# Agent attention with a gated convolution: one 2560-column DMA transpose for both query units of a pair

## The chip, the cores and the metric

One core of a Trainium2 chip. The metric is the device time of one execution in microseconds; the time shown is the median of three runs.

## The reference

Four batches of 12800 rows with 128 channels, and 49 agents. Attention runs twice: agents over keys and values give a 49 x 128 matrix per batch, then each query row attends to the 49 agents. The result x goes through a causal convolution of 5 taps (a sum over taps per channel), a sigmoid, a product with `x @ w_val`, and a last projection.

```python
a2k = sm(agents, k);  agent_v = a2k @ v          # sm: scaled scores, softmax over the last axis
q2a = sm(q, agents);  x = q2a @ agent_v
for kk in range(5):
    gate_pre += conv_w[kk] * xp[:, kk:kk + S, :]  # xp: x with 4 zero rows ahead
out = (sigmoid(gate_pre) * (x @ w_val)) @ w_out
```

## The kernel before

`agent_v` is folded with the taps and weights into small stationary matrices (`stat`), so that x itself is never formed. The work on queries goes by units of 1280 rows (40 in all, number g), in five steps:

1. `queries`: score matmuls on TensorE (line 376), a 32x32 block transpose (386) and row maxima (745) on VectorE, subtraction on GpSimd (750), exp on ScalarE (758), sums and normalisation on VectorE (763 to 772). The probabilities of a unit are then written three times in 16 bits into a buffer `pt` of [128, 10, 128]: the high part by ScalarE (779), copies of two thirds of it by GpSimd (784), and the low rest by GpSimd (794).
2. `transposes`: `pt` is turned over, so that the 128 entries of a query row lie along the partitions. The first four units do it on TensorE; units 4 to 39 by a DMA transpose, issued by SyncE (835). Its destination is half of an `x1` buffer. An `x1` buffer holds a segment: two units, 2560 columns, segment s = units 2s and 2s+1. There are four `x1` buffers and four `pt` buffers.
3. `shifts`: two plain DMAs per segment (884, from segment 2 on) copy some rows of `x1` at five column offsets into `x2`. They read both halves of the segment. `halo` (819) copies the last 4 columns of the segment before by GpSimd.
4. `gates` and `values`, by chunks of 512 columns (five to a segment, chunk t belongs to segment t // 5): five matmuls on `x1` (922) and one on `x2` (926) give the gate, two more (949, 953) the value. ScalarE applies tanh (935), VectorE multiplies (962), ScalarE rounds to `hh` (968), GpSimd forms the rest `hl` (973).
5. `project`: three matmuls (992 to 994, the last with `hl`), a scaled copy to `ob` on ScalarE (1006), and an output store per pair of chunks (1021).

Loads of keys, queries and values (369) go through 11 buffers `ld`; a load waits until TensorE has used what lay in its buffer. All loads, stores, shifts and DMA transposes are issued by SyncE, in one queue.

TensorE's order is written out by hand (`order`, line 1088). The order on the other engines and on the DMA queue is set by a planner, `Plan`: each step is added with an engine, a duration, what it reads and writes, and for a DMA the time on the wire (`moved`). `Plan.order` walks through a modelled time and picks the next step of each engine by the longest chain behind it (`tail`). The durations are only used for this order.

Of the kernel before, what the change touches and what calls it, by code (L numbers as in the profile page):

```python
# [10 lines left out]
F16 = mybir.dt.float16  # L11
# [6 lines left out]
P = 128  # L18
# [5 lines left out]
NBLK = 10  # L24
# [5 lines left out]
PAD = 16  # L30
# [10 lines left out]
NPT = 4  # L41
NX = 4
# [25 lines left out]
class Plan:  # L68
# [11 lines left out]
    def add(self, engine, us, fn, reads=(), writes=(), moved=0.0, key=None, urge=0.0):  # L80
        i = len(self.steps)
        need = set()
        for x in reads:
            need |= self.wrote.get(x, set())
        for x in writes:
            need |= self.wrote.get(x, set()) | self.read.get(x, set())
        for x in reads:
            self.read.setdefault(x, set()).add(i)
        for x in writes:
            self.wrote[x], self.read[x] = {i}, set()  # L90
        self.steps.append((engine, us, fn, need, moved, key))
        self.urge.append(urge)
# [84 lines left out]
def tile_agent_attention_gated_conv(  # L177
# [25 lines left out]
    def ring(n, shape, dtype, name, pool=const):  # L203
        return [pool.tile(shape, dtype, name=f"{name}{i}") for i in range(n)]
# [12 lines left out]
    qw = ring(NPT, [P, NBLK, A], F32, "qw")  # L217
    qsm = ring(2, [P, NBLK], F32, "qsm")
    qr = ring(2, [P, NBLK], F32, "qr")
    pts = ring(NPT, [P, NBLK, P], F16, "pt")  # L220
    x1s = ring(NX, [P, PAD + SEG], F16, "x1_")
    x2s = ring(3, [P, SEG], F16, "x2")
    ths = ring(NT_, [P, CH], F32, "th")
# [25 lines left out]
    def bank():  # L249
        turn[0] += 1  # L250
        i = turn[0] % 2
        return sc[i], ("sc", i)
# [13 lines left out]
        out=fold, in0=ident[:, 0:AP_], in1=ident[:, AP_:P], op=ALU.add  # L266
# [246 lines left out]
    def fold_weights(b):  # L513
# [143 lines left out]
        def transposes():  # L657
# [4 lines left out]

        add(
            "pe", 0.6, transposes, [(*w_, n) for n in "derv"] + [(*w_, "g")], [at_w],
            key="m",
        )
# [132 lines left out]
    def on_pe(b, u):  # L799
        g = b * NU + u  # L800
        return g < PE_FIRST or (g < (B - 1) * NU and g % TURN in PE_TURNS)

    def unit_rows(g):
        o = PAD + g % 2 * UNIT
        return x1s[g // 2 % NX][:, o : o + UNIT]
# [21 lines left out]
    def transposes(b, u):  # L827
        g = b * NU + u
        pt = pts[g % NPT]
        p_ = ("pt", g % NPT)  # L830
        if not on_pe(b, u):
            dst = unit_rows(g)
            add(
                "dma", 1.4,
                lambda: nc.sync.dma_start_transpose(
                    out=dst.rearrange("p (n i) -> p n i", i=P),
                    in_=pt.rearrange("p n r -> p (n r)"),
                ),
                [(*p_, n) for n in range(3)], [("x1", g // 2 % NX, g % 2)], 2.4,
            )  # L840
            shifts(b, u)
            return
        ps_, at = bank()
        ps = ps_.rearrange("p a b -> p (a b)").bitcast(F16).rearrange("p (h w) -> p h w", h=2)
        dst = unit_rows(g).rearrange("p (h w) -> p h w", h=2)

        def matmuls():
            for n in range(NBLK):
                nc.tensor.transpose(
                    out=ps[:, n // HB, n % HB * P : (n % HB + 1) * P], in_=pt[:, n, :],  # L850
                    identity=ident16,
                )

        add("pe", 0.65, matmuls, [("pt", g % NPT, n) for n in range(3)], [at], key="t")
        add(
            "act", 0.65, lambda: nc.scalar.copy(out=dst[:, 0], in_=ps[:, 0, 0 : HB * P]),
            [at], [("x1", g // 2 % NX, g % 2)],
        )
        add(
            "dve", 0.46,  # L860
            lambda: nc.vector.tensor_copy(out=dst[:, 1], in_=ps[:, 1, 0 : HB * P]),
            [at], [("x1b", g // 2 % NX, g % 2)],
        )
        shifts(b, u)

    def shifts(b, u):

        g = b * NU + u
        if g >= SINGLE and g % 2 == 0:
            return  # L870
        n = 1 if g < SINGLE else 2
        u0 = u + 1 - n
        s = g // 2
        x2, x1 = x2s[s % 3], x1s[s % NX]
        o = (g + 1 - n) % 2 * UNIT
        src = row_keys(s, range(0, g % 2 + 1))
        c = PAD - HALO + o
        for r0, r1, every, us in X2CUTS:
            first = A + (2 if every == 3 else 3 * THREES)
            rows = x1[first : first + 1 + (r1 - r0 - 1) * every : every, c : c + 1]  # L880
            view = [rows.ap[0], (1, TAPS), (1, n * UNIT)]
            add(
                "dma", 0.6,
                lambda r0=r0, r1=r1, rows=rows, view=view: nc.sync.dma_start(
                    out=x2[r0 * TAPS : r1 * TAPS, o : o + n * UNIT],
                    in_=bass.AP(rows.tensor, rows.offset, view),
                ),
                src, [("x2", s % 3, o + i * UNIT, r0) for i in range(n)], us * n,
            )
        if g % 2 and (g + 1) // 2 < B * NU // 2:  # L890
            halo((g + 1) // 2)
# [165 lines left out]
    for b in range(B):  # L1057
        t0 = b * NCH
        for i in range(NU):
            g = b * NU + i + LEAD  # L1060
# [61 lines left out]
    def gate_and_state(t):  # L1122
        state[t] = gates(t)

    run = {
        "k": key_scores, "v": agent_values, "q": queries, "t": transposes,
        "max": lambda b: step(key_max, b), "fold": lambda b: step(fold_weights, b),
        "g": gate_and_state, "a": values, "o": project,
# [58 lines left out]
```

## Time and profile before

| | |
|---|---|
| median of 3 runs | 427.45 us (426.17 to 427.92) |
| span of the profiled execution | 423.6 us |
| its own time | not listed apart from the span; the median lies 3.85 us above the span |
| TensorE busy | 403.9 us (95%) |
| VectorE, ScalarE, GpSimd busy | 293.3, 301.5, 228.2 us |
| bytes moved by DMA | 127.62 MB, mean 301 GB/s |
| DMA transposes (x<-pt) | 36, issued by SyncE |

The span is the time from the first to the last instruction. The page's rows of 40 digits cut it into slices of 10.6 us. In a timeline, the first number is the start and the second the length in us; `SPq` rows are issues on SyncE, and their length is the time of the issue, not of the transfer. In a row of windows, the last three numbers are the granted TensorE clock, the busy share of the DMA engines and GB/s.

### The profile page before, as it was taken

Reading aid. Unit: us, or ns where it says so; the run is one execution under the profiler, and the core shown is the slowest. Engines: PE = TensorE matmul, PEld = TensorE weight load, DVE = VectorE, ACT = ScalarE, POOL = GpSimd, SP = SyncE. Lnnn points to the kernel's source line nnn. Section 1 sums busy time; section 2 is a strip of 40 time slices with the busy share of each in tenths; the row PEclk is TensorE's granted clock in tenths of the full one; section 3 lists DMA queues with packets and bytes.
Section 4 is the critical chain, followed back from the end, with each engine's and each line's share of the span. In section 5 each row is a group of like instructions: output and inputs, shape, how many; then the busy total and the mean of one; then the engine's idle time right before and its main releaser. Section 6 shows DMA issues by size and latency. Waiting matters only on the chain.

```text
span 423.6 us, 10042 instructions
## 1 busy us (share of the span) xinstructions
PE 403.9 (95%) x3907; PEld 197.0 (47%) x3907; DVE 293.3 (69%) x562; ACT 301.5 (71%) x521; POOL 228.2 (54%) x263
## 2 busy tenths in 40 slices
PE   4979999999999999999999899999999989999995
PEld 1358434346555443446555343335555534344443
DVE  3757899867875978667795575767765678676231
ACT  1564568779966777678876486778876567788776
POOL 1002557654657565554566355574366277877553
PEclk9969999999999999999999899999999999999998
DMA  8999999999999999999999999999999977755733
GB/s 320 420 417 411 370 367 353 301 295 310 412 293 283 346 317 362 304 278 356 351 379 324 271 299 370 314 332 302 296 393 322 239 196 161 199 163 176 205 121 124
DMA packets 75129, 127.62 MB, mean 301 GB/s; under 512 B 50466, under 2 KB 50850, under 8 KB 75084
## 3 DMA queue, kind: packets, MB, share of 16 engines
q1 hardware_dynamic: 74940, 126.87, 96.9%
q8 instruction: 30, 0.49, 0.5%
q10 hardware_dynamic: 144, 0.13, 0.2%
q14 instruction: 15, 0.12, 0.1%
HBM read 79.25 MB, written 26.21 MB: 249 GB/s over the span
## 4 chain that ended last, share of the span: by engine, by line
PE 78%; DMA 9%; DVE 8%; ACT 1%; POOL 1%; issue 1%; SPq 0%; POOLq 0%; DVEq 0%; ACTq 0%
PE gate L922 23%; PE sc L376 17%; PE av L480 10%; PE val L949 5%; PE out L992 5%; PE val L953 5%; PE gate L926 5%; PE out L993 4%; DMA ld<-kT 4%; PE out L994 4%; DMA x<-pt 3%; DMA x<-x 2%; DVE h L962 1%; DVE qw L772 1%; DVE qsm L763 1%
## 5 line engine op out<-in xcount | busy, mean ns | idle before, releaser
L973 POOL TENSOR_TENSOR hl<-h,hh 128x512 f16<-128x512 f32 (+1 forms) x101 | 116.9, 1158 | 96.1 <-ACT hh L968 96.0
L922 PE MATMUL gate<-x,stat 128*128 128x512 f16 (+1 forms) x500 | 125.2, 380 | 0.2 <-ACT th L935 0.2
L962 DVE SCALAR_TENSOR_TENSOR h<-th,val 128x512 f32<-128x512 f32 x100 | 67.8, 678 | 66.8 <-PE out L993 26.2
L376 PE MATMUL sc<-ld,ag_sb 128*32 128x320 f32 x1280 | 101.5, 447 | 7.6 <-DMA ld<-kT 7.0
L935 ACT ACTIVATE th<-gate,unscale 128x512 f32<-128x512 f32 x100 | 68.3, 683 | 33.3 <-PE gate L926 31.7
L1006 ACT ACTIVATE ob<-out,oscale 128x512 f32<-128x512 f32 x98 | 67.3, 687 | 21.3 <-PE out L994 20.1
L922 PEld LDWEIGHTS <-stat 128*128 128x128 f16 x505 | 46.3, 97 | 63.7 <-issue 14.8
L968 ACT CAST hh<-h 128x512 f16<-128x512 f32 (+1 forms) x101 | 61.5, 609 | 17.2 <-DVE h L962 16.4
L750 POOL TENSOR_TENSOR qw<-sT,qmx 128x490 f32<-128x490 f32 x40 | 41.4, 1035 | 47.6 <-DVE qmx L745 47.5
L376 PEld LDWEIGHTS sc<-ld,ag_sb 128*32 128x32 f32 x1280 | 36.7, 111 | 59.4 <-issue 25.7
L480 PE MATMUL av<-ld,eT 128*32 128x129 f32 (+1 forms) x1400 | 50.7, 279 | 1.0 <-DVE eT L386 1.0
L480 PEld LDWEIGHTS av<-ld,eT 128*32 128x32 f32 (+1 forms) x1400 | 47.1, 117 | 7.5 <-issue 2.5
L794 POOL TENSOR_TENSOR pt<-qw,pt 128x490 f16<-128x490 f32 x40 | 44.8, 1120 | 3.1 <-ACT pt L779 2.9
L471 ACT ACTIVATE e<-ks,kbias 128x320 f32<-128x320 f32 x80 | 39.3, 554 | 5.4 <-DVE eT L386 3.3
L386 DVE STREAM_TRANSPOSE sT<-sc 128x640 f32<-128x640 f32 x40 | 33.6, 839 | 13.4 <-PE sc L376 12.7
L402 ACT COPY ks<-sc 128x640 f32<-128x640 f32 x40 | 27.7, 691 | 21.2 <-PE sc L376 19.1
L386 DVE STREAM_TRANSPOSE eT<-e 128x640 f32<-128x640 f32 x40 | 33.5, 842 | 9.8 <-ACT e L471 5.2
L926 PE MATMUL gate<-x,stat 95*128 95x512 f16 x100 | 38.3, 383 | 1.5 <-DMA x<-x 1.5
L949 PE MATMUL val<-x,stat 128*128 128x512 f16 x100 | 38.2, 382 | 0.8 <-DVE h L962 0.6
L953 PE MATMUL val<-x,stat 95*128 95x512 f16 x100 | 38.1, 381 | 0.0
L994 PE MATMUL out<-hl,wo 128*128 128x512 f16 x98 | 37.0, 378 | 1.1 <-POOL hl L973 1.1
L992 PE MATMUL out<-hh,wo 128*128 128x512 f16 x98 | 37.3, 381 | 0.1
(130 smaller groups left out, 389.4 us busy)
## 6 DMA issues: line engine op xcount, KB each, us to landing
ld<-kT SPq DMA_DIRECT2D x40, 640.0 KB
ld<-qT SPq DMA_DIRECT2D x40, 640.0 KB
ld<-vP SPq DMA_DIRECT2D x39, 645.0 KB
outT<-ob SPq DMA_DIRECT2D x48, 512.0 KB
x<-x SPq DMA_DIRECT2D x18, 375.0 KB
x<-x SPq DMA_DIRECT2D x18, 100.0 KB
outT<-ob SPq DMA_DIRECT2D x3, 256.0 KB
x<-x SPq DMA_DIRECT2D x4, 187.5 KB
```

The source lines that it names most:

```text
L376: nc.tensor.matmul(out=out[g * BLK : (g + 1) * BLK, j, 0:GT], lhsT=ag_sb[:, b, j * BLK : (j + 1) * BLK], rhs=src[:, g * GT : (g + 1) * GT] ...
L386: nc.vector.transpose(out=out.rearrange("p n (j i) -> p j n i", j=2), in_=in_.rearrange("p j (n i) -> p j n i", i=BLK),)
L480: nc.tensor.matmul(out=av[o + j : o + j + cols, 0 : C + 1], lhsT=et[:, n, j : j + cols], rhs=vt[:, n, :], start=(u == 0 and n < 2), stop=( ...
L922: nc.tensor.matmul(out=pg, lhsT=stat[:, k, :], rhs=x1[:, c : c + w], start=(k == 0), stop=False,)
L926: nc.tensor.matmul(out=pg, lhsT=stat[0 : TAPS * X2R, TAPS + 1, :], rhs=x2[0 : TAPS * X2R, o2 : o2 + w], start=False, stop=True,)
L935: lambda: nc.scalar.activation(out=th, in_=pg, func=AF.Tanh, scale=unscale[:, 0:1]),
L949: nc.tensor.matmul(out=pv, lhsT=stat[:, TAPS, :], rhs=x1s[(b * NCH + n0 // CH) // 5 % NX][:, PAD + o2 : PAD + o2 + w], start=True, stop=False,
L953: nc.tensor.matmul(out=pv, lhsT=stat[0 : TAPS * X2R, TAPS + 2, :], rhs=x2[0 : TAPS * X2R, o2 : o2 + w], start=False, stop=True,)
L962: lambda: nc.vector.scalar_tensor_tensor(out=h, in0=th, scalar=1.0, in1=pv, op0=ALU.add, op1=ALU.mult),
L968: "act", 0.16 + 0.42 * scale, lambda: nc.scalar.copy(out=hh, in_=h),
L973: lambda: nc.gpsimd.tensor_tensor(out=hl, in0=h, in1=hh, op=ALU.subtract),
L1006: lambda: nc.scalar.activation(out=ob[:, o : o + w], in_=po, func=AF.Copy, scale=oscale),
```

## The change

The two `pt` buffers of a pair become two halves of one buffer `ptp` of [128, 2, 10, 128]. The even unit issues no transpose; the odd one issues a single DMA transpose of all 2560 columns into the whole `x1` buffer. It reads all three parts of both units and writes both halves. In the planner it has 2.6 us of issue (1.4 before, for each of two) and 3.6 us on the wire (2.4 before, for each of two). Shifts, gates and `halo` are as before.

```diff
-    pts = ring(NPT, [P, NBLK, P], F16, "pt")
+    ptp = ring(NPT // 2, [P, 2, NBLK, P], F16, "pt")
+    pts = [t[:, h] for t in ptp for h in range(2)]
...
         if not on_pe(b, u):
-            dst = unit_rows(g)
+            if g % 2 == 0:
+                return
+            s = g // 2 % NX
+            pair = ptp[g // 2 % (NPT // 2)]
             add(
-                "dma", 1.4,
+                "dma", 2.6,
                 lambda: nc.sync.dma_start_transpose(
-                    out=dst.rearrange("p (n i) -> p n i", i=P),
-                    in_=pt.rearrange("p n r -> p (n r)"),
+                    out=x1s[s][:, PAD:].rearrange("p (n i) -> p n i", i=P),
+                    in_=pair.rearrange("p h n r -> p (h n r)"),
                 ),
-                [(*p_, n) for n in range(3)], [("x1", g // 2 % NX, g % 2)], 2.4,
+                [("pt", i % NPT, n) for i in (g - 1, g) for n in range(3)],
+                [("x1", s, 0), ("x1", s, 1)], 3.6,
             )
             shifts(b, u)
             return
```

Five lines come into the file, so line 835 becomes 839, 884 becomes 889, 1021 becomes 1026, and 369 becomes 370. TensorE's order is the same row for row. On the other engines the planner, fed with the new step, sets a new order in parts. Names below: `ld` are load buffers, `x_0` to `x_3` the `x1` buffers, other `x` the `x2` buffers; in the new kernel a `pt` is the buffer of a pair.

SyncE's queue at segment 2 (units 4 and 5), the first with DMA transposes, before:

```order
L369 DMA ld_70<-qT 128x1280
L835 DMA_TRANSPOSE x_2_103<-pt_97 128x10x128
L369 DMA ld_71<-vP 128x1290
L835 DMA_TRANSPOSE x_2_103<-pt_98 128x10x128
L369 DMA ld_61<-vP 128x1290
L1021 DMA outT<-ob_121 128x1024
L369 DMA ld_62<-vP 128x1290
L884 DMA x_107<-x_2_103 75x1x2560
```

and now:

```order
L370 DMA ld_70<-qT 128x1280
L370 DMA ld_71<-vP 128x1290
L370 DMA ld_61<-vP 128x1290
L839 DMA_TRANSPOSE x_2_101<-pt_97 128x20x128
L1026 DMA outT<-ob_119 128x1024
L370 DMA ld_62<-vP 128x1290
L370 DMA ld_63<-qT 128x1280
L889 DMA x_105<-x_2_101 75x1x2560
```

The transpose moved behind two value loads, and one more load (`ld_63`) stands between it and the shifts.

The same queue at segment 9 (units 18 and 19), before:

```order
L835 DMA_TRANSPOSE x_1_102<-pt_99 128x10x128
L369 DMA ld_71<-kT 128x1280
L835 DMA_TRANSPOSE x_1_102<-pt_100 128x10x128
L1021 DMA outT<-ob_123 128x1024
L369 DMA ld_61<-kT 128x1280
L369 DMA ld_62<-qT 128x1280
L884 DMA x_105<-x_1_102 75x1x2560
L884 DMA x_105<-x_1_102 20x1x2560
L835 DMA_TRANSPOSE x_2_103<-pt_97 128x10x128
```

and now:

```order
L370 DMA ld_71<-kT 128x1280
L370 DMA ld_61<-kT 128x1280
L839 DMA_TRANSPOSE x_1_100<-pt_98 128x20x128
L1026 DMA outT<-ob_121 128x1024
L370 DMA ld_62<-qT 128x1280
L370 DMA ld_63<-kT 128x1280
L889 DMA x_103<-x_1_100 75x1x2560
L889 DMA x_103<-x_1_100 20x1x2560
L370 DMA ld_64<-qT 128x1280
```

Two key loads stand ahead of the transpose, a key load more ahead of the shifts (`ld_63`), and no transpose directly behind them. At segment 4 two loads more stand ahead of the shifts.

GpSimd's queue at unit 32, near 330 to 341 us of the profile, before:

```order
L784 TENSOR_SCALAR pt_97<-qw_89 128x10x30
L794 TENSOR_TENSOR pt_97<-qw_89,pt_97 128x10x49
L819 COPY x_0_101<-x_3_104 128x4
L973 TENSOR_TENSOR hl_117<-h_111,hh_114 128x512
L973 TENSOR_TENSOR hl_118<-h_112,hh_115 128x512
L541 TENSOR_TENSOR gw<-avT,moe_sb 128x245
```

and now:

```order
L785 TENSOR_SCALAR pt_97<-qw_89 128x10x30
L795 TENSOR_TENSOR pt_97<-qw_89,pt_97 128x10x49
L978 TENSOR_TENSOR hl_115<-h_109,hh_112 128x512
L820 COPY x_0_99<-x_3_102 128x4
L978 TENSOR_TENSOR hl_116<-h_110,hh_113 128x512
L542 TENSOR_TENSOR gw<-avT,moe_sb 128x245
```

The halo copy, which reads the end of the segment before, moved behind the first of the two `hl`.

## The prediction

> **What bounds the kernel now.** I read the head of the page first, then the waits of the matmul engine, then the chain of waits around the one long wait, then the sync engine's timeline.
>
> ```profile
> span 423.6 us, 10042 instructions
> PE 403.9 (95%) x3907; PEld 197.0 (47%) x3907; DVE 293.3 (69%) x562; ACT 301.5 (71%) x521; POOL 228.2 (54%) x263
> PEclk9969999999999999999999899999999999999998
> DMA  8999999999999999999999999999999977755733
> PE sc L376 <- DMA ld<-kT: 7.0, 4, 6.1
> PE gate L926 <- DMA x<-x: 1.5, 1, 1.5
> PE out L994 <- POOL hl L973: 1.1, 1, 1.1
> ```
>
> TensorE is busy for 95% of the span, so it is the bound. The 7.0 us on key loads are the start, which the change leaves alone; TensorE waits for no load after it. Behind it there are two waits of over 1 us: 1.5 us on a shift copy and 1.1 us on GpSimd's `hl`. The DMA row says something else that matters here: for 32 of 40 slices the wire is full as well. It seldom stops TensorE, since loads run far ahead; it reaches TensorE only where a transfer is wanted soon after it is issued. That is the path of this change: transposes, then shifts, then the gate matmul L926. The 1.5 us lie there, in segment 9 (units 18 and 19):
>
> ```profile
> 220.73 7.50 DMA x<-pt
> 228.28 7.34 DMA x<-x
> 235.67 0.39 PE gate L926
> 236.89 2.24 PE gate L922 x5
> ...
> 243.56 1.19 PE gate L922 x5
> ```
>
> The second transpose is issued at 220.73, has landed 7.50 us later, the shifts go out at 228.28, and land 7.34 us after that. The five gate matmuls behind the wait take 2.24 us, those at 243.56 take 1.19. The granted clock says why:
>
> ```profile
> 237.00:240.40 3.40, 3.40 (x9) 1.17 (x8) 1.99 (x7) 1.30 (x2) 1.84 (x3) 0.50 1.05 335
> ```
>
> The eighth column is the clock: 0.50 for 3.4 us after the 1.5 us wait, so half of 3.4, 1.7 us, is lost beside it. The 1.1 us wait of L994 was followed by no such spell (in the page's clock row the only 8 behind the start and ahead of the end is slice 23, 233 to 243.6 us; 340 lies in a slice with 9). Segment 9 costs 1.5 + 1.7 = 3.2 us today. The sync queue around it:
>
> ```profile
> 212.77 7.23 SPq L835 DMA_TRANSPOSE x<-pt  x1
> 220.10 0.53 SPq L369 DMA_DIRECT2D ld<-kT  x1
> 220.73 2.63 SPq L835 DMA_TRANSPOSE x<-pt  x1
> 223.45 1.47 SPq L1021 DMA_DIRECT2D outT<-ob  x1
> 225.02 0.38 SPq L369 DMA_DIRECT2D ld<-kT  x1
> 225.49 0.73 SPq L369 DMA_DIRECT2D ld<-qT  x1
> 228.28 1.65 SPq L884 DMA_DIRECT2D x<-x  x2
> 213.83 0.45 POOL L784 TENSOR_SCALAR pt<-qw 128x300 f16<-128x300 f32 x1
> ```
>
> The odd unit's buffer is complete at 213.83 + 0.45 = 214.3, yet its transpose is issued at 220.7: the first issue takes 7.23 us, since the queue behind it is full. So what decides the landing is not readiness but the bytes queued ahead, at the wire's rate.
>
> **The change, part by part.** TensorE's order is the same row for row, so its work is unchanged; only its waits can move.
>
> Readiness: the merged transpose of segment 9 can be issued at 214.3 instead of 212.8. The 1.5 us cost nothing, because the wire has 7 us queued at that moment; where that cover is gone they would be paid in full. Issue time: two quiet issues and one wire rate:
>
> ```profile
> 361.24 2.94 SPq L835 DMA_TRANSPOSE x<-pt  x2
> 112.00:120.00 8.00, 8.00 (x84) 3.94 (x83) 5.95 (x10) 6.64 (x13) 6.41 (x7) 1.00 1.02 418
> ```
>
> One merged issue should take about the 2.94 us of two; nothing is won or lost. At 418 GB/s (last column) a load of 128x1280 floats, 0.655 MB, takes 1.6 us. This prices the moves. The order puts one more load ahead of segment 9's shifts (the key load after the query load), so they land 1.6 us later. In segment 2 it is also one load, in segment 4 two. Behind the waiting merged transpose stand an output store and loads; that no load is waited for after the start covers their delay, and without that cover a load late by 1.5 us would be a wait of 1.5 us.
>
> What a transpose costs the wire beyond its bytes is the large term. Stretches from the first to the last transposed packet of a pair, with rows in the order segments 4, 5 (transposes adjacent), 2, 9 (a load between) and 17 (quiet):
>
> ```profile
> 120.90:127.06 6.16, 6.16 (x111) 3.86 (x103) 5.04 (x9) 3.22 (x7) 3.49 (x6) 1.00 1.23 199
> 131.61:137.65 6.04, 6.04 (x113) 4.10 (x102) 4.57 (x13) 2.81 (x6) 4.01 (x4) 1.00 1.23 182
> 77.77:85.69 7.92, 7.92 (x58) 3.06 (x57) 7.08 (x13) 6.55 (x13) 4.72 (x6) 1.00 1.16 289
> 220.04:227.72 7.68, 7.68 (x89) 4.13 (x82) 4.29 (x8) 5.25 (x10) 4.79 (x6) 1.00 1.21 242
> 362.44:365.74 3.30, 3.30 (x21) 1.27 (x23) 1.10 (x2) 2.72 (x6) 3.30 (x4) 1.00 1.12 230
> 120.90:124.50 3.60, 3.60 (x99) 2.70 (x91) 2.86 (x5) 1.64 (x4) 2.73 (x4) 1.00 1.24 223
> ```
>
> Lost time is length x (1 - rate/418): 6.16 x (1 - 199/418) = 3.2 us in segment 4, 3.4 in segment 5, 2.4 in segment 2, 3.2 in segment 9, 1.5 in the quiet one; the mean of the four loaded pairs is 3.1. A merged transpose loses between 1.5 (no partner, no queue) and 3.4 (two in a row under load). The first transpose of segment 4 alone, the last row, loses 3.60 x (1 - 223/418) = 1.7; that is engines coming into step. The second loses as much again, though the engines are in step already; I put that down to the hand-over between two instructions, which the merged one has not. So I take the first one's 1.7 and half the quiet pair's 1.5 for the second half: 2.4 us, 0.7 below the mean, both ends kept. By segment 9 eight pairs have passed: 8 x 0.7 = 5.6 us less on the wire, with ends 8 x 1.6 = 12.8 less and 8 x 0.3 = 2.4 more.
>
> The Trainium skill (DMA: Bandwidth & Descriptors, "Anatomy of one DMA") gives each DMA a fixed 2.0 us, fitted for another issuing path, and its rules for kernel authors say to coalesce. Taken as wire time, that is an estimated 16 us by segment 9; segments 2 and 4 would then not wait, and the sum below would be 1.2 us lower. The row at 112:120, with 418 GB/s through queued DMAs, does not bear it out: beside other transfers a fixed part is hidden.
>
> Now the tight segments, with these rows:
>
> ```profile
> 86.20 1.68 SPq L884 DMA_DIRECT2D x<-x  x2
> 93.97 0.38 PE L926 MATMUL gate<-x,stat 95*128 95x512 f16 x1
> 127.74 1.67 SPq L884 DMA_DIRECT2D x<-x  x2
> 135.69 0.38 PE L926 MATMUL gate<-x,stat 95*128 95x512 f16 x1
> ```
>
> Segment 2: shifts issued at 86.20 land at about 93.5 if they take 9's 7.34 us (an estimate), 0.4 before L926. One load more (+1.6), its own pair losing 2.4 as before (0): they land at 95.1, a new wait of 1.2 us. Ends: 0, if they land faster than 7.34 since no transpose follows them directly any more, and 1.6. Being at the 1.1 us that brought no half-clock spell, I count none; 1.7 if it does.
>
> Segment 4: 127.74 + 7.34 = 135.1, due 135.7. Two loads (+3.2) less what segments 3 and 4 save (2 x 0.7) give 136.9; TensorE, 1.2 late, comes at 136.9. Wait 0, ends 0 and 2.0.
>
> Segment 9: landing at 235.6 + 1.6 - 5.6 = 231.6; TensorE wants it at 235.67 - 1.5 + 1.2 = 235.4. No wait, no spell: -3.2. This holds as long as the eight pairs save over about 1 us together.
>
> The wait of L994 on `hl`:
>
> ```profile
> 338.78 0.19 POOL L819 COPY x<-x 128x4 f16<-128x4 f16 x1 [5.99 <-DMA x<-pt]
> 338.93 2.27 POOL L973 TENSOR_TENSOR hl<-h,hh 128x512 f16<-128x512 f32 x2
> 340.13 0.38 PE L994 MATMUL out<-hl,wo 128*128 128x512 f16 x1 [1.11 <-POOL hl L973]
> ```
>
> GpSimd waits 5.99 us for a transpose before its halo copy, with two `hl` behind it; L994 needs the first. In the new order that `hl` stands ahead of the copy, so the 1.11 us go, unless the second becomes late in turn (the merged transpose lands later). Between 0 and -1.1: I take -0.6.
>
> Other reordering on ScalarE, VectorE and GpSimd keeps each unit's steps within one or two chunks of their places; I cost it at nothing, covered by TensorE's queue of other chunks, and if that cover fails it is a wait like the 1.1 us one. The buffers' second use is tight only at segment 9:
>
> ```profile
> 229.62 0.61 ACT L779 CAST pt<-qw 128x490 f16<-128x490 f32 x1 [0.40 <-DVE qw L772]
> ```
>
> This write into unit 18's old place now needs the whole merged transpose landed; today's second one has by 228.3. One load ahead and 5.6 saved make it 224.3: free.
>
> Sum: +1.2 + 0 - 1.5 - 1.7 - 0.6 = -2.6 us; span 421.0. The shown median, 427.45, lies 3.85 above the profiled span, so 427.45 - 2.6 = 424.9, or -0.6%. What a measurement of this kernel can tell from no change is 0.5%, 2.1 us.
>
> **The rivals.**
>
> Same time: the spell moves instead of going. Segment 2's wait of 1.2 to 1.6 us lies between 1.1 (no spell) and 1.5 (spell). If it draws one, +1.7: 426.6. If besides `hl` stays late, 427.2. For it: the wait sits right at the unknown threshold. Against: its shifts have no transpose behind them any more. 427 as its middle.
>
> Slower: the merged transpose loses more wire time than its two parts. Place: segments 2 to 9, price eight times the difference. Wire and TensorE meet at segment 9: with 3.4 us lost per pair (segment 5's) the shifts land at 235.6 + 1.6 + 2.4 = 239.6, 4.0 later than now, the spell stays, and the buffer's write on ScalarE, due at 229.62, waits for 228.3 + 1.6 + 2.4 = 232.3: 427.45 + 4.0 = 431.4. It decides once a merged one loses 0.1 more than the mean: 1.6 + 8 x 0.1 = 2.4 us. For it: both adjacent pairs above lose the most of all. Against: they are still two instructions.
>
> Faster still: with 1.6 us saved per pair (the quiet end) and shifts landing sooner with no transpose behind them, segment 2 waits 0 and `hl` gives all: -3.2 - 1.1 = -4.3, 423.1. For it: the quiet pair's 1.5 us. Against: the wire is never quiet before slice 33. The Trainium skill's fixed cost (above) points this way.
>
> That nothing changes on the queue is out: the order has 18 transposes of 2560 columns for 36 of 1280.
>
> **How the numbers follow.** Forecast 424.9: 0.34. Faster still, 423.1: 0.09. Same, 427: 0.31. Slower, about 431: 0.26. Faster by over 0.5% is 0.34 + 0.09 = 0.43, within 0.31, slower 0.26. The range goes from 422.0, just below the 423.1 case, to 431.5, the slower case at its priced value; about 2 in 10 lie beyond, mostly above. The likeliest case's own range is 423.5 to 426.
>
> **What would show it.** Right: no wait of L926 on x<-x at chunk 45, no 0.50 clock stretch near 237, a wait near 1 us at chunk 10, shorter stretches of transposed packets (pairs under 5.5 us), no wait of L994 on `hl` near 340. Wrong: the same wait at chunk 45 with later shifts; ScalarE's L779 waiting for x<-pt; new waits of L926 in segments 8 or 14; half-clock stretches at new places.

## The result and the profile after

| | before | after |
|---|---|---|
| median | 426.81 us (425.42 to 427.92, 4 runs) | 438.67 us (438.15 to 439.27, 4 runs) |
| ratio | 1 | 1.0272, 95% interval 1.0229 to 1.0315 |
| span of the profiled execution | 423.6 us | 435.7 us |

The change makes the kernel 2.7% slower, outside the range of the prediction and on the other side of the forecast. Ratios, here and below, leave out single runs that lie over 1.5% above the fastest of their kernel; medians and ranges keep them. The head of the page of the kernel after:

```profile
span 435.7 us, 9982 instructions
PE 404.5 (93%) x3907; PEld 195.3 (45%) x3907; DVE 291.0 (67%) x562; ACT 300.5 (69%) x521; POOL 227.9 (52%) x263
PEclk9989999987999999999999999999999999999999
DMA  8999999999999999999899999999999968555733
```

TensorE is busy for 404.5 us, nearly as before (403.9), so nearly all of the 12.1 us is added waiting. The clock row has a new low place, its 9th and 10th digits, and the start ran faster (8 for 6 in the third digit), which hides the new spell in the busy time. The 8 that stood at the 23rd is gone, since that spell now falls on two slices. The waits of TensorE, in us in total, times and longest:

```profile
PE gate L931 <- DMA x<-x: 10.2, 3, 5.0
PE sc L377 <- DMA ld<-kT: 7.0, 5, 5.9
PE av L433 <- DVE m L426: 2.0, 1, 2.0
PE val L954 <- DVE h L967: 1.4, 1, 1.4
...
PE gate L927 <- ACT th L940: 1.2, 2, 1.1
```

The wait on the shifts has grown from 1.5 us in one piece to 10.2 in three; the wait of L994 (now L999) on `hl` is gone; a wait on the key maximum `m` and one on tanh are new. The third piece, 1.01 us, lies at segment 0 and is not the change's: a second profile of the kernel before has 1.14 us there. The other two, and the waits between them, by TensorE's timeline (start, length, in brackets the wait ahead):

```profile
98.69 0.61 PE L931 MATMUL gate<-x,stat 95*128 95x512 f16 x1 [4.97 <-DMA x<-x]
...
190.78 1.24 PE L927 MATMUL gate<-x,stat 128*128 128x512 f16 x5 [1.05 <-ACT th L940]
...
195.34 0.27 PE L433 MATMUL av<-ident,m 128*2 128x128 f32 x1 [2.01 <-DVE m L426]
...
248.44 0.38 PE L931 MATMUL gate<-x,stat 95*128 95x512 f16 x1 [4.25 <-DMA x<-x]
```

98.69 is chunk 10, the first of segment 2 (93.97 before, 4.7 us earlier); 248.44 is chunk 45, segment 9 (235.67 before, 12.8 earlier). Two windows of the clock, in the columns of the prediction:

```profile
95.64:102.47 6.83, 3.78 (x41) 1.92 (x45) 0.81 (x1) 3.01 (x6) 1.16 (x1) 0.50 1.19 212
249.24:252.65 3.41, 3.41 (x12) 1.50 (x11) 2.07 (x7) 1.07 (x3) 1.54 (x2) 0.50 0.80 160
```

The first is new: 3.78 us of work at half clock, 1.9 lost. The second is the one the kernel before had at 237, moved by 12.2. So 4.7 of the 12.1 us are there at chunk 10, 1.9 follow by its spell, 3.1 come at 190 to 196, and 2.75 (4.25 - 1.5) at chunk 45; the `hl` wait gives 1.1 back, and smaller waits make up the rest (1.4 us on `h` for 0.6 before).

Now the path to chunk 10. SyncE's queue at segment 2, first before, then after:

```profile
73.26 5.94 SPq L835 DMA_TRANSPOSE x<-pt  x1
79.30 0.52 SPq L369 DMA_DIRECT2D ld<-vP  x1
79.94 2.68 SPq L835 DMA_TRANSPOSE x<-pt  x1
82.71 0.53 SPq L369 DMA_DIRECT2D ld<-vP  x1
83.34 0.38 SPq L1021 DMA_DIRECT2D outT<-ob  x1
83.81 0.40 SPq L369 DMA_DIRECT2D ld<-vP  x1
```

```profile
77.06 8.95 SPq L839 DMA_TRANSPOSE x<-pt  x1
86.12 0.51 SPq L1026 DMA_DIRECT2D outT<-ob  x1
86.73 0.38 SPq L370 DMA_DIRECT2D ld<-vP  x1
87.20 0.90 SPq L370 DMA_DIRECT2D ld<-qT  x1
88.19 1.71 SPq L889 DMA_DIRECT2D x<-x  x2
```

Between the last transpose and the shifts stand a store and two loads in both orders; the load more of the new order is the one ahead of the transpose. The shifts are issued at 88.19, 2.0 us later than in this profile of before; the prediction had 1.6 for their delay. This part is not firm: in the nine profiles below whose queue up to there is that of before, the shifts are issued at 86.2 to 88.4. And the merged issue holds SyncE for 8.95 us, and the store and loads behind it are issued at 86.1 to 88.1, right ahead of the shifts; before they went out at 82.7 to 84.2, with 2 to 3.5 us to spare. The stretch from the shifts' issue to their landing, before and after:

```profile
86.20:93.67 7.47, 7.40 (x45) 3.10 (x45) 5.52 (x10) 5.26 (x11) 3.49 (x5) 1.00 1.10 306
```

```profile
88.19:98.64 10.45, 5.45 (x25) 2.09 (x22) 4.84 (x8) 4.96 (x9) 2.71 (x4) 0.86 1.17 263
```

10.45 us instead of 7.47. The wire moved 2.75 MB instead of 2.29, which at 306 GB/s is 1.5 us; the other 1.5 us are the lower rate, 263 GB/s. The length is firm: 10.26 and 10.35 us in two more profiles of this order, 7.15 to 9.15 in the nine with the queue of before. Segment 9, by the chain of waits:

```profile
224.75 13.61 DMA x<-pt
...
238.42 9.97 DMA x<-x
```

The transpose lands at 238.36. TensorE was ready for chunk 45 at 248.44 - 4.25 = 244.19, 5.8 us later; before, the second transpose landed 5.9 us ahead of that point (228.22 and 234.17). So here too the transpose is not late against TensorE; the shifts are, 9.97 us instead of 7.34. This piece is less firm than chunk 10: of three runs below with the same queue at segment 9, two have shifts of 7.5 and 7.6 us there, one of 10.0.

The waits at 190 to 196 begin on GpSimd and pass through ScalarE:

```profile
188.35 0.19 POOL L820 COPY x<-x 128x4 f16<-128x4 f16 x1 [6.87 <-DMA x<-pt]
188.50 1.01 POOL L751 TENSOR_TENSOR qw<-sT,qmx 128x490 f32<-128x490 f32 x1
...
189.54 0.61 ACT L759 ACTIVATE qw<-qw 128x490 f32<-128x490 f32 x1 [4.58 <-POOL qw L751]
```

The halo copy waits 6.87 us for segment 7's transpose, the subtraction of the queries stands behind it, ScalarE's exp waits 4.58 us for that, and tanh and the key copies stand behind the exp.

### The profile page after: what moved, and what is told of

Its sections match the earlier page's. It is cut to its first block, busy times and chain, and to the rows that moved or that the text cites. A ratio compares the mean times of both kernels' runs of the same rounds, so it can differ in the third digit from the quotient of the medians.

```text
span 435.7 us, 9982 instructions
## 1 busy us (share of the span) xinstructions
PE 404.5 (93%) x3907; PEld 195.3 (45%) x3907; DVE 291.0 (67%) x562; ACT 300.5 (69%) x521; POOL 227.9 (52%) x263
## 4 chain that ended last, share of the span: by engine, by line
PE 69%; DMA 22%; DVE 4%; ACT 1%; issue 1%; POOL 1%; SPq 1%; POOLq 0%; DVEq 0%
PE gate L927 20%; PE sc L377 15%; DMA x<-pt 8%; PE av L481 7%; DMA x<-x 6%; DMA ld<-vP 6%; PE val L954 4%; PE gate L931 4%; PE out L997 4%; PE val L958 4%; PE out L998 4%; PE out L999 4%; DMA ld<-kT 2%; DVE h L967 1%; DVE qsm L764 1%
## 5 line engine op out<-in xcount | busy, mean ns | idle before, releaser
L377 PE MATMUL sc<-ld,ag_sb 128*32 128x320 f32 x1280 | 103.0, 451 | 8.0 <-DMA ld<-kT 7.0
L481 PEld LDWEIGHTS av<-ld,eT 128*32 128x32 f32 (+1 forms) x1400 | 45.4, 115 | 9.4 <-issue 3.7
L931 PE MATMUL gate<-x,stat 95*128 95x512 f16 x100 | 38.5, 385 | 10.2 <-DMA x<-x 10.2
L412 DVE TENSOR_REDUCE kmx<-ks 128x2 f32<-128x640 f32 x39 | 31.5, 812 | 8.4 <-ACT ks L403 8.3
```

The source lines that it names most:

```text
L377: nc.tensor.matmul(out=out[g * BLK : (g + 1) * BLK, j, 0:GT], lhsT=ag_sb[:, b, j * BLK : (j + 1) * BLK], rhs=src[:, g * GT : (g + 1) * GT] ...
L481: nc.tensor.matmul(out=av[o + j : o + j + cols, 0 : C + 1], lhsT=et[:, n, j : j + cols], rhs=vt[:, n, :], start=(u == 0 and n < 2), stop=( ...
L931: nc.tensor.matmul(out=pg, lhsT=stat[0 : TAPS * X2R, TAPS + 1, :], rhs=x2[0 : TAPS * X2R, o2 : o2 + w], start=False, stop=True,)
```

## The experiments

Each time is a median, each ratio is against runs of the kernel before on the same chip. "Order" is the order of every engine's instructions.

**Order, instruction and place: three runs.** They tell apart the merged instruction (theory A), the planner's order (B) and the place of the first half (C). The first keeps the order of the kernel after and splits the instruction again:

```diff
-    nc.sync.dma_start_transpose(out=x1s[s][:, PAD:]..., in_=pair...)
+    for h in range(2):
+        nc.sync.dma_start_transpose(out=unit_rows(g - 1 + h)..., in_=pair[:, h]...)
```

> The changed kernel's order on every engine, but at each place of the merged transpose two transposes of 1280 columns back to back, from the two halves of the same buffer. Theory A (the single long instruction delays what is queued behind it): back near the kernel before, 427 to 429 us, with no wait of L926 above 2 us. Theory B (the planner's new order, with a load more between transpose and shifts in segments 2 and 9, is what costs): 437 to 440, the waits at chunks 10 and 45 as in the changed kernel. Theory C (the first half no longer starts before the second unit is ready): 437 to 440 too, since the first half still waits for the second here.

Measured: 438.75 us (434.24 to 442.11), ratio 1.0241 (1.0163 to 1.032). In time the same as merged. The trace is not: TensorE waits 5.26 us at chunk 10, much as merged (4.97), but hardly at chunk 45,

```profile
245.83 0.39 PE L936 MATMUL gate<-x,stat 95*128 95x512 f16 x1 [0.57 <-DMA x<-x]
```

and there are half-clock spells at 195.3 (3.41 us) and 355.7 (6.83 us) and a wait of 2.07 us on tanh instead. The second keeps the order of the kernel before; the planner gets its old two steps, the even one issues nothing:

```diff
     add("dma", 1.4,
-        lambda: nc.sync.dma_start_transpose(out=dst..., in_=pt...),
+        merged,            # the odd unit issues 2560 columns, the even one nothing
         [(*p_, n) for n in range(3)], [("x1", s, g % 2)], 2.4)
```

> The order of the kernel before on every engine, row for row; only the even unit's transpose is gone and the odd unit's place issues the merged one of 2560 columns. Theory A (the instruction): 436 to 440 us. Theory B (the planner's order): 424 to 428. Theory C (the first half starts late): 434 to 440, with the transposes landing later after the odd unit's issue than in the kernel before, where 9's landed 7.5 us after it.

Measured: 431.93 us (431.32 to 435.45), 1.0152 (1.0101 to 1.0204). The third is the second with two transposes at the odd unit's place:

> As the run with the merged transpose in the order of before, but two transposes of 1280 columns back to back at the odd unit's place. Theory A (the instruction): 427 to 429 us, since there is no long instruction. Theory B (the planner's order): 425 to 428. Theory C (the first half starts late): 434 to 440, the same as with the merged one.

Measured: 431.82 us (429.96 to 433.29), 1.0131 (1.0086 to 1.0175). Both times lie between the ranges that I had given to the three theories, above 429 and below 434, so no theory holds alone. The merged instruction is worth nothing that can be seen in either order (438.67 and 438.75; 431.93 and 431.82): A falls. The place of the first half costs 1.3 to 1.5%, some 6 us, and the planner's order another 1.2% by the ratios, some 5 us (6.7 by the medians). Both B and C hold, each for about half. One thing in my expectations was wrong: split, the first half waits only for its own unit, and its place in the queue, not the second unit, makes it late.

The third run shows what the place alone does. SyncE's queue in it at segment 2, and from its chain of waits the shifts:

```profile
75.23 9.63 SPq L841 DMA_TRANSPOSE x<-pt  x2
84.96 0.54 SPq L370 DMA_DIRECT2D ld<-vP  x1
85.59 0.38 SPq L1031 DMA_DIRECT2D outT<-ob  x1
86.06 0.38 SPq L370 DMA_DIRECT2D ld<-vP  x1
86.93 1.69 SPq L894 DMA_DIRECT2D x<-x  x2
```

```profile
86.93 9.31 DMA x<-x
```

Against the kernel before, the first transpose and one value load have changed places, nothing else. The shifts are issued 0.7 us later, and take 9.31 us instead of 7.47; what stands between is issued at 85 to 86.4 instead of 82.7 to 84.2. That fits SyncE's hold as the cause, but it does not show it. The four profiles with a late first half in the order of before have 8.69 to 9.41 us for these shifts, and the nine with the queue of before 7.15 to 9.15: longer on average by 1.2 us, with ranges that overlap. No run takes the hold away by itself. In this trace TensorE waits 2.61 us at chunk 10, with a spell of 6.83 us behind it, and 2.89 us on `hl` at 344.72, with one of 3.41; chunk 45 doesn't wait. So that the first half's place costs some 6 us is shown; by which wait it does so changes from run to run.

**Shifts ahead of what stands between.** The queue of the kernel after, with the store and two loads moved behind the shifts in segments 2 and 9:

> The changed kernel, but in segments 2 and 9 the store and the two loads that stood between transpose and shifts stand behind the shifts. If the shifts are late because of what is queued between (theories A and B, in their part on the queue), they land about 4 us after their issue instead of 10, the waits of L926 at chunks 10 and 45 go, and with them the half-clock spells: 438.7 less 5.0, 4.3 and about 3 of spells is 427 us, with something of it lost again where the wire stands idle. If they are late because the transposes themselves land late (theory C), they still wait at least 2 us each: 434 or more.

Measured: 446.46 us (444.4 to 447.64), 1.0471 (1.0427 to 1.0516): the worst of all. The shifts did land sooner, 6.1 us after their issue in both segments, and the waits at chunks 10 and 45 fell to 0.80 and 0.49 us. But the waits only moved:

```profile
PE gate L935 <- DMA x<-x: 8.3, 4, 5.9
PE out L1001 <- ACT ob L1015: 2.7, 1, 2.7
PE gate L931 <- DMA x<-pt: 2.1, 1, 2.1
```

The longest, 5.9 us, lies at segment 4 now, whose transpose took 14.28 us to land. I read this as a wire that is full anyway, where what is put back comes late for everything behind it; no run isolates that.

**One segment's place.** The order of before, merged in segments 3 to 19 alone, then in segment 2 alone. The first of the two, against the second run above:

```diff
-                if g % 2:
+                if s == 2 and g < 6:    # segment 2: a transpose for each unit, as before
+                    nc.sync.dma_start_transpose(out=unit_rows(g)..., in_=pt...)
+                elif g % 2:
```

> The order of before on every engine, with merged transposes at the odd units' places in segments 3 to 19; segment 2 keeps its two transposes at their old places. If the price of the late first half sits in segment 2 (wait of 2.65 us at chunk 10 and a half-clock spell of 3.4 us that costs 1.7): 431.9 - 4.3 = 427.6 us, and no wait at chunk 10. If it is spread over later segments, the waits at chunk 45 (3.5 us) and on hl (3.9 us) stay and the time is 429 to 432.

Measured: 429.66 us (427.38 to 436.21), 1.0055 (1.0019 to 1.0092).

> The kernel before, order and all, with the merged transpose in segment 2 alone. If the late first half does its harm there (shifts land 2.6 us later, and a half-clock spell behind the wait): 429 to 431 us, with a wait of 2 to 3 us at chunk 10. If not: 426 to 428.

Measured: 428.44 us (426.34 to 430.95), 1.0055 (1.0025 to 1.0086). Segment 2 carries a part: undoing it there gives 2.3 us back by the medians (431.93 to 429.66; 1.0%, some 4 us, by the ratios), doing it there alone costs 2.0 (426.46 beside it), between the two cases expected. My 4.3 is not excluded by the first, but the second is below it, and the wait at chunk 10 didn't go in the first of the two (1.6 us). The rest is elsewhere: that run waits 3.60 us at chunk 45 and 1.27 on `hl`.

**One load in the order.** The kernel after, in segment 2 the last load ahead of the shifts moved behind them:

> The changed kernel with one edit in the queue: in segment 2 the query load that the planner put ahead of the shifts stands behind them. If a load ahead of the shifts costs its wire time there (1.6 us), they land 8.8 us after their issue instead of 10.45, the wait at chunk 10 falls from 5.0 to about 3.3 us, and the time from 438.7 to 436 (437 without, 435 with a shorter half-clock spell). If the shifts are late for what stands directly behind the transpose (the first load took 3.3 us there instead of 1.6), the wait stays above 4.5 us and the time at 438 to 439.

Measured: 435.59 us (434.57 to 438.35), 1.0193 (1.0135 to 1.0252), 3.1 us less. As expected of the load's own wire time:

```profile
97.05 0.39 PE L935 MATMUL gate<-x,stat 95*128 95x512 f16 x1 [3.16 <-DMA x<-x]
```

The wait falls from 4.97 to 3.16 us, and the shifts take 8.75 us. The waits behind it are not those of the kernel after, though: 3.33 us at chunk 20, where there was none, and 0.87 at chunk 45 for 4.25. So the 3.1 us are not the load at chunk 10 alone.

**The planner's two numbers.** The kernel after with two numbers changed:

```diff
-                "dma", 2.6,  ...  3.6,
+                "dma", 9.0,  ...  6.0,
```

> The changed kernel with two other numbers in the planner and nothing else: the merged transpose has 9.0 us of issue and 6.0 us on the wire there, about what the trace of the changed kernel shows under load (2.6 and 3.6 before). If the planner's order is what makes the changed kernel slower than the merged one in the old order, another order moves the time by several us, and with truer numbers down: 428 to 434. If any order with the merged transpose loses the same: 437 to 440.

Measured: 430.31 us (427.56 to 434.03), 1.0061 (1.0022 to 1.01). Two numbers that only set the order are worth 8.4 us. What stood on the shifts is now on loads, which the new order puts later:

```profile
PE gate L931 <- DMA x<-x: 2.5, 2, 1.6
PE av L481 <- DMA ld<-vP: 1.6, 2, 1.4
PE sc L377 <- DMA ld<-qT: 1.4, 1, 1.4
```

**The halo copy.** GpSimd's order alone: each halo copy up to four of its steps later, ahead of the gate that reads it. In the kernel after, in the kernel before, and in the merged one in the order of before:

```diff
+    for h in halos:      # h: the planner's halo step of a segment
+        a = seq.index(h)
+        pool = [n for n in range(a, len(seq)) if plan.steps[seq[n]][0] == "pool"]
+        need = [n for n in range(a, len(seq)) if h in plan.steps[seq[n]][3]]
+        z = min(pool[min(4, len(pool) - 1)], min(need) - 1)
+        seq[a : z + 1] = seq[a + 1 : z + 1] + [h]
```

> The changed kernel; only GpSimd's order differs: each halo copy stands up to four GpSimd steps later, still ahead of the gate matmul that reads it. If the halo copy's wait for the later transpose (6.9 us at 188.35) holds up GpSimd's other work and through it ScalarE and VectorE, TensorE's waits at 190.8 (1.05 us, on tanh) and 195.3 (2.0 us, on the key maximum) go, and perhaps the 1.4 us at 358.6: 438.7 - 3 to 4.5 = 434 to 436. The waits at chunks 10 and 45 stay. If those waits have another cause, or TensorE only meets the shifts of segment 9 earlier: 438 to 439.

Measured: 435.29 us (433.76 to 436.26), 1.0189 (1.0144 to 1.0233), 3.4 us less. The waits of 1.05 us on tanh and 2.0 us on `m` are gone, and GpSimd has no wait on a transpose left; the wait at chunk 45 is 5.69 us now, since TensorE comes sooner.

> The kernel before with the same edit on GpSimd's order alone. If the halo copy is what makes hl late, the wait of 1.1 us of L994 near 340 goes and the time falls by about 1 us, to 425.9. If not, no change, 427.

Measured: 423.59 us (421.34 to 425.23), 0.9911 (0.9874 to 0.9949): faster than the kernel before by 3.3 us, three times what I expected. In its profile the wait on `hl` is gone, and so are the 1.5 us at chunk 45 and the spell behind them.

> The merged transpose in the order of before (431.9 us), with the halo copies later on GpSimd. Its wait of 3.95 us on hl and the half-clock spell behind it (1.7 us) go, if the halo copy's wait for the transpose (9.7 us, the longest of that run) causes them: 426 to 428. If the waits on the shifts (2.7 and 3.5 us) are all that matters: 431 to 432.

Measured: 427.85 us (425.12 to 431.5), 1.002 (0.9989 to 1.0052), 4.1 us less than without. So the halo copy is worth 3.3 to 4.1 us in all three kernels; it is a loss of the kernel before as well, and not what the change costs.

**The order, once more.** The kernel after with both edits, halo copies later, and one load put back in segments 2 and 9:

> The changed kernel with two edits: in segments 2 and 9 the last load ahead of the shifts stands behind them, and the halo copies stand later on GpSimd. If these two are all that the planner's order costs, the time is that of the merged transpose in the order of before with the halo copies later, 427 to 429 us. With 3.1 for the load in segment 2 alone and nothing for the one in segment 9: 432. If something else in the order costs: 433 or more.

Measured: 429.55 us (428.33 to 431.56), 1.0098 (1.0064 to 1.0131). It lies just above the 427 to 429 of the first case and below the other two. Of the 7.4 us between the two orders with late halo copies (435.29 and 427.85) the two loads are 5.7 by the medians, and of the 1.7% by the ratios 0.9%. What is left, 1.7 us or 0.8%, stays open.

**What merging is worth without both.** The order of before, late halo copies, two transposes in segment 2, merged ones behind:

> The order of before, merged transposes in segments 3 to 19, two at their old places in segment 2, and the halo copies later on GpSimd. If the late first half costs only through segment 2 and the halo copy, this is as fast as the kernel before with the halo copies later, 423.6 us (423 to 425), and merging itself is worth nothing. If the merged transposes save wire, 420 to 422. If they cost elsewhere (segment 9), 426 to 428.

Measured: 427.36 us (424.15 to 431.19), 1.0012 (0.9973 to 1.0051): the last of the three cases. It is not as fast as 423.59:

```profile
PE gate L944 <- DMA x<-x: 3.6, 3, 3.0
```

The 3.0 us are at chunk 45. With segment 2 put right, TensorE comes earlier and waits at segment 9 instead. The late first half costs about 4 us in segments 3 to 19 alone, as much as in all of them (427.85).

**The kernel before itself.** A second profile:

> The kernel before itself, a second profile: how much its own tight places move from one execution to the next. If the profile shown is typical, no wait of L926 at chunk 10, 1.5 us at chunk 45, 1.1 us on hl. If segment 2 lies at the edge in the kernel before too, as the run that edits only segment 9 suggests (2.0 us at chunk 10 there), a wait of 1 to 2 us may appear at chunk 10 and a half-clock spell with it.

Measured: 424.79 us, one run.

```profile
95.20 0.38 PE L926 MATMUL gate<-x,stat 95*128 95x512 f16 x1 [0.99 <-DMA x<-x]
```

TensorE does wait at chunk 10, though no spell follows. The 0.3 us of room that the first profile showed there were one execution's; in the other runs with this queue up to there, the wait was between under 0.8 and 2.4 us. Chunk 45 moves as much:

```profile
235.78 0.39 PE L926 MATMUL gate<-x,stat 95*128 95x512 f16 x1 [0.38 <-DMA x<-x]
```

The first profile had 1.5 us there and a half-clock spell; here there are 0.38 us and no spell, at nearly the same span (422.8 and 423.6 us). The 3.2 us that the prediction set out to win were in good part that execution's.

**Shifts first in the kernel before.** Segment 9 alone, a try for a faster kernel:

> The kernel before with one edit in the queue: in segment 9 the shifts stand directly behind the second transpose, the store and two loads behind them. With nothing ahead shifts took 6.1 us from issue to landing in the run with shifts first; so they land at 228.3 + 6.1 = 234.4 instead of 235.6, the wait of 1.5 us at chunk 45 falls to 0.3 or less, and the half-clock spell behind it (1.7 us) goes: 426 - 2.9 = 423 us. Rival: the loads put back leave the wire idle for some 3 us, and a later segment waits for its transposes, as in the run with shifts first: 428 or more.

Measured: 431.43 us (429.02 to 433.65), 1.0102 (1.0069 to 1.0134). The wait at chunk 45 went, as expected, and the rival holds for the time. I put the loss down to a halo copy that waited 8.4 us:

> The kernel before with the halo copies later on GpSimd (423.6 us) and, in segment 9, the shifts directly behind the second transpose. If shifts first cost the kernel before 4.5 us through the halo copy (it waited 8.4 us at 265.95 for a later transpose, with the queries' subtraction behind it), that loss is gone here and only the gain at segment 9 stays: 421 to 423.5. If the loss is the wire's (the load and the store put back), it stays: 426 to 428.

Measured: 429.67 us (427.8 to 431.61), 1.0081 (1.0053 to 1.011), above both cases. One halo copy still waited 3.1 us, so a last pair with up to eight steps:

> The kernel before with the shifts of segment 9 directly behind the second transpose, and the halo copies up to eight GpSimd steps later. If the halo copy's wait was what cost the two runs with shifts first (431.4 and 429.7), it is gone: 421 to 424. If it is the store and the loads put back (ScalarE waits for the store's buffer, keys come late), 427 to 430.

Measured: 427.3 us (425.82 to 431.11), 1.0033 (1.0006 to 1.0059). Without the shifts first:

> The kernel before with the halo copies up to eight GpSimd steps later, nothing else. With four steps the copy hardly waited any more (0.7 us in all), so no more is to be had: 423 to 424. If a later copy makes the gate matmul wait for it, 425 or more.

Measured: 422.96 us (420.76 to 428.34), 0.9891 (0.9859 to 0.9922). This pair is 4.3 us apart; with four steps it was 6.1 (429.67 and 423.59), without the halo copies' move 4.6 (431.43 and 426.87). With the halo waits gone, the edit costs as much as before: my reason falls. The run with shifts first waits 2.52 us for shifts at chunk 60, with a half-clock spell at its end, which fits what is put back on the wire; that is not shown. The last kernel is the fastest of all, 1.1% faster than the kernel before.

## Why the prediction was wrong

In the terms of its sum: the step that failed is the price of nothing for the late first half (its readiness and its issue), which the second and third runs measure at 1.3 to 1.5%, some 6 us; next to it, the new order, priced at +1.2 us for a load and -0.6 on `hl`, costs 1.2%, some 5 us. The gain that was to pay for both, 1.5 + 1.7 us at segment 9, didn't come. Part by part:

**TensorE's work** unchanged: right. **Wire saved**: right in kind. The four stretches of the prediction, in the order segments 4, 5, 2, 9, for merged transposes:

```profile
127.33:133.30 5.97, 5.97 (x110) 3.80 (x103) 5.13 (x11) 2.64 (x6) 1.57 (x2) 1.00 1.21 192
145.62:149.35 3.73, 3.73 (x51) 1.44 (x47) 3.52 (x15) 2.76 (x6) 1.28 (x2) 1.00 1.34 238
80.94:87.63 6.69, 6.69 (x60) 2.36 (x53) 5.31 (x9) 5.24 (x9) 5.58 (x7) 1.00 1.24 254
231.80:237.86 6.06, 6.06 (x29) 2.72 (x28) 5.89 (x11) 4.44 (x8) 5.02 (x6) 1.00 1.26 175
```

By the same working they lose 3.2, 1.6, 2.6 and 3.5 us, a mean of 2.7 where the prediction took 2.4 and the pairs before lost 3.1. That this is the merging isn't shown: two transposes back to back in the order of the kernel after took as long in segment 9,

```profile
231.66:237.66 6.00, 6.00 (x63) 3.06 (x56) 5.55 (x11) 4.90 (x9) 4.31 (x5) 1.00 1.27 165
```

so a hand-over between two instructions, on which I based the 0.7, does not show there. Over all eight segments from 2 to 9, by the same working, the pairs before lose 23.8 us, the merged ones 20.3 and the two back to back in the same order 20.7: 3.5 us less instead of 5.6, with or without merging. The engines coming into step and the hand-over are my readings of such lengths; no run shows either by itself.

**"8 x 0.7 = 5.6 us less on the wire" by segment 9**: failed, together with the wait and spell of 3.2 us that it was to remove (0.38 us and no spell in the second profile of the kernel before). Saved wire time did not bring the landing forward, because a transpose can't be issued before its unit is ready, and the unit is ready when TensorE has come so far. In segment 9 the unit's last write ends at 224.72, the transpose's issue is at 224.75:

```profile
222.59 2.13 POOL L795 TENSOR_TENSOR pt<-qw,pt 128x490 f16<-128x490 f32 x2 [0.16 <-ACT pt L780]
```

Before, the odd unit's buffer was complete at 214.3; TensorE was some 10 us late by then, so the transpose was too.

**"The 1.5 us cost nothing, because the wire has 7 us queued"** and **"nothing is won or lost" on the issue**: failed. In segment 2 the transpose did land about as the forecast would have it (88.1; 86.2 + 1.6 = 87.8), but under load a merged issue holds SyncE for 8.95 and 10.23 us (2.94 us was the quiet price), and everything behind it is issued only then. In the kernel before the two issues hold it as long together (5.94 and 2.68 us in segment 2, 7.23 and 2.63 in segment 9), but the first one's hold came earlier, with a load issued between. That this is how the late first half costs is argued, as said above. I named the store and the loads that stand behind the transpose, and asked whether anyone waits for them; I didn't ask what stands behind those: the shifts.

**Shifts in 7.34 us**: 10.45 and 9.97 (the second 7.5 and 7.6 in the two other runs). **Segment 2, +1.2 us and no spell**: right in place and sign, 4.97 us and 1.9 of spell in size; the extra load was seen, at 1.6 us (without one load the wait falls by 1.8). **Segment 4, no wait**: right. **`hl`**: gone, as forecast; **Other reordering at nothing**: failed, the same halo copy now blocks GpSimd at 188 instead, for 3.1 us of waits. The slower rival had the sign, not the mechanism: by these rows the merged transpose loses no more wire time than its parts (2.7 us for 3.1).

The Trainium skill (DMA: Bandwidth & Descriptors, "Rules for kernel authors") says to coalesce many small transfers into one large one. The halves here, 128 x 1280 x 2 bytes = 0.33 MB, are not small, and the runs show no gain: 438.67 us merged, 438.75 as two.

## What to carry to other kernels

A step that is moved later in one in-order queue can cost through everything that stands behind it, not only through what it delays itself: ask when the queue is free again, and who waits for the last in the row. A wait of 1.5 us in one profile is no gain to count on: take a second profile of the kernel before. Before a planner's order is put down to the change, feed the old order to the new instruction; here nearly half of the loss was the order, and two of the planner's numbers were worth 8.4 us. A tiny copy that waits for a transfer at the head of an in-order engine is worth moving: the halo copies, 1 us by the waits that name them, gave 3.3 us.

## What was not expected of the hardware

The half-clock spells don't follow the length of a wait alone. In the second run (merged, order of before), a wait of 3.49 us at chunk 45 was followed by full clock, where 1.5 us had brought a spell in the kernel before:

```profile
241.87:245.28 3.41, 3.40 (x18) 1.82 (x19) 1.98 (x7) 1.94 (x3) 0.73 (x1) 1.00 1.16 318
```

Behind the start, waits of up to 1.4 us never brought one, and waits of 1.62, 2.03 and 2.42 us in three other runs didn't either. Ahead of the end, the spells last 3.41 us or a multiple of it, and within a run their starts lie whole multiples of that apart: 95.64 and 249.24 in the kernel after (45 times 3.413), 96.95 and 349.54 in the second run (74 times). The wait of 3.49 us falls across such a point, 240.31, with 1.93 us of it ahead and 1.56 behind; each part is longer than the 1.5 us that brought a spell, so that alone doesn't explain it, and what decides stays open. The Trainium skill (TensorE: Matmul & The Clock Gate, "Part 1: The HAM clock gate") has the clock fall after an idle window of about 3.4 us; the lengths agree with that window; the wait of 1.5 us that brought a spell in the kernel before was shorter than it.
